# Chunked attention and two gated products on one core: operand parts and weight sums made ahead of the bursts

## The chip, the cores and the metric

The kernel runs on one core of a Trainium2 chip. The metric is the device time in microseconds (us) of one execution, the median over several runs. Five engines work side by side: TensorE (PE, with its weight loads as PEld), VectorE (DVE), ScalarE (ACT), GpSimd (POOL) and SyncE (SP). SP and POOL issue most of the transfers. Each engine runs its instructions in the order in which the program gives them to it, and waits at an instruction until what it needs is there.

## The reference

```python
# q, k, v: (8, 8, 576, 64) float32; 4608 tokens of 512 features
scores = q_c @ k_c^T / sqrt(64)                 # chunks of 64 tokens
attn   = softmax(scores, axis=-1)
x = (attn @ v_c) rearranged to (4608, 512)
x = ((x @ w_a) * (x @ w_b)) @ w_out             # d_ff 1536
out = (((x @ w1) * (x @ w2)) @ w3) @ w_out2     # d_ff 1024
```

## The kernel before

**Numbers.** A float32 operand is split into a high part and a rest, and each product is three matmuls of such parts (`SEQ`). A split is a cast on ACT (L287) and a subtraction on DVE or POOL (L288), both in `split`.

**Tiles and stages.** The 4608 tokens are nine blocks of 512. Phase 0 is the first gated product (d_ff 1536: twelve slices of 128), phase 1 the second (eight slices), with w3 and w_out2 multiplied together once. In phase 0 blocks 0 and 1 are done by `plain_step` (L1041): PE makes pa and pb (L901), DVE multiplies them (L1061 for block 1, into the tile G0p; L1065 for block 0), and `Second` (L925) multiplies with a slice of w_out (L944, twelve matmuls). The weights are converted meanwhile (`Pump`): float32 copies go to DRAM as `d`, split ones as `dw` and `dwo`, by stores on POOL. The last four plain steps are block 0's slice 11 and block 1's slices 9, 10 and 11; they are called the plain tail here. Blocks 2 to 7 run as three pairs per phase (phase 1 has four), by Strassen's scheme in `strassen_step` (L982): seven products P5, P1, P2, P6, P3, P7, P4 a slice instead of eight (L914).

**What a pair needs first.** Its x parts, by `strassen_pieces` (L605): four differences of x tiles ("formed", L616) and seven splits ("one"), each for two halves, 22 pieces in all. For the first pair also weight sums: class `Sums` (L809) loads `d` of a slice (L819, tile su), makes four sums on DVE (L827 to L830), splits two of them into w tiles and stores them as `dw[..][2]` and `[3]` (POOL) for the later pairs, which load all four parts by `load_part` (L794).

**Bursts.** After a pair's last step, and after the plain steps, `burst` (L1084) multiplies the second block's slices with w_out: twelve slices of twelve matmuls each. Beside it the x parts of the next pair are made (`Track(others, ...)`), and from its fifth slice on the attention of the pair after next goes on. `back(order)` makes the burst begin with slices 10 and 11 and then go down. The w_out slices lie in four tiles (`Outs`, L758); a slice's load (L782, tile wo) is put into the program three or four slices ahead. The first one that burst 1 loads is wo_7, for its fifth slice.

**Order of the loads.** All these loads go out on SP, one behind the other in program order; each waits at its head for its buffer and for its source's store. Attention's q, k and v loads (tiles qk and v, L181) are queued by `ask` and handed out a few at a time by `tick` and `settle`. While `state["hold"]` is true none is handed out; `burst` sets it at its start and clears it after its first slice.

Of the kernel before, what the change touches and what calls it, by code (L numbers as in the profile page):

```python
# [17 lines left out]
P = 128  # L18
NT = 512
# [91 lines left out]
def chunk_attention_two_gated_products(  # L111
# [493 lines left out]
    def strassen_pieces(x32, nm, single=False, diffs=None):  # L605
# [8 lines left out]
        def minus(a, b, name):  # L614
            t = diffs.popleft() if diffs else tmp(name, W)
            nc.vector.tensor_tensor(t, a, b, op=ALU.subtract)  # L616
            return t
# [23 lines left out]
        def one(p, kt):  # L641
# [5 lines left out]
        order = [  # L647
            (formed, "P5"),
            (formed, "P6"),
            (one, "P5"),  # L650
            (one, "P1"),
            (one, "P2"),
            (formed, "P7"),
            (one, "P6"),
            (formed, "P4"),
            (one, "P3"),
            (one, "P7"),
            (one, "P4"),
        ]
        return parts, [  # L660
            (0.7, False, lambda do=do, p=p, kt=kt: do(p, kt)) for do, p in order for kt in range(2)
        ]

# [145 lines left out]
    class Sums:  # L809
# [63 lines left out]
        def early(self, i):  # L873
            t = w_tile(6 + i, f"w{self.ph}_{self.f}_s{i}")
            self.parted(i, t)

# [207 lines left out]
    def burst(ph, j, order, gplaces, others, at, first=None):  # L1084

        n = NF[ph]
        order = back(order)
        sums = []
        state["banks"] = ("acc2", "acc3")
        track = Track(others, 2 * n // 3, engines)  # L1090
        state["hold"] = True
        parts = [ready(ph, j, order[0], gplaces) if first is None else first]
        parts.append(ready(ph, j, order[1], gplaces))
        state["outs"].ahead(3)
        for f in range(n):
            if f and f + 2 < n:
                parts.append(ready(ph, j, order[f + 2], gplaces))
            s = Second(ph, j, f, state["outs"].next(), parts[f], sums, ("rC", "rA", "rB", "rD"))
            s.part()
            s.part()  # L1100
            track.point()
            if f > 3:
                for a in at:
                    a.point()
            s.rest()
            if f == 0:
                state["pending"].rest()
                parts.append(ready(ph, j, order[2], gplaces))
                state["hold"] = False
            state["outs"].ahead(3 if f else 4)  # L1110
        track.finish()
        state["pending"], state["banks"] = None_(), ("rB", "rD")
# [88 lines left out]
    with tc.manual_schedule():  # L1201
# [83 lines left out]
        AHEAD = 5  # L1285
# [86 lines left out]
        at = None  # L1372
        for n, (T, f) in list(enumerate(order))[1:]:
# [9 lines left out]
            def point(pe=True):  # L1383
                if conv:
                    conv.point(pe)
                (at or late).point(pe)

            if T == 1:
                for i in [f + 1] if f else [0, 1]:
                    for m in range(2 if i < NF[0] else 0):  # L1390
                        store(dw[0][i][m], whole(pairs[0, i][m]).bitcast(F32), 2, nc.gpsimd)
            if n + 3 == len(order):
                at.finish()
                next_units(2)
                state["pace"] = 9
            if n + 1 == len(order):
# [5 lines left out]
        at.finish()  # L1402

# [15 lines left out]
        def block_steps(ph, sb, x, at):  # L1419
# [10 lines left out]
            for k, f in enumerate(order):  # L1430
                extra = None
                if new:
                    if k + 2 < n:
                        su[k + 2] = summed(ph, order[k + 2], k + 2)
                        su[k + 2].load()
                    extra = Track(su[k + 1].pieces() if k + 1 < n else [], 5, engines, 2.0)
# [7 lines left out]
                def freed(i):  # L1444
                    if k + 2 < n:
                        if whole_new and f + 2 >= READY:
                            return
                        if not new or i in (0, 3):
# [10 lines left out]
                if k + 1 == n and ph == 0 and sb + 1 < NSB:  # L1459
                    for a in at:  # L1460
                        a.finish()
                    next_units(sb + 2)
# [67 lines left out]
        for ph, sb in [(0, sb) for sb in range(1, NSB + 1)] + [(1, sb) for sb in range(NSB + 1)]:  # L1530
# [13 lines left out]
            elif not begins:  # L1544
                x, pieces = strassen_pieces(x32, f"{ph}{sb}", sb == NSB)
            if ph == 0 and sb == 1:
                for n_ in range(2):
                    first_sums[n_] = summed(ph, orders[ph, sb][n_], n_)
                    first_sums[n_].load()
                    for i in (0, 3):  # L1550
                        load_part(ph, orders[ph, sb][n_], i)
                pieces = pieces + first_sums[0].pieces()
# [54 lines left out]
            j, places = block_steps(ph, sb, x, at)  # L1607
# [51 lines left out]
```

## Time and profile before

| what | us |
|---|---|
| median of 3 runs | 1606.45 |
| lowest to highest | 1604.29 to 1608.12 |
| the profiled execution | 1609.44 |
| its span on the core | 1607.6 |
| PE busy | 1545.6 (96% of the span) |
| DVE busy | 859.0 (53%) |
| ACT, POOL busy | 538.4, 492.6 (33%, 31%) |

The span is what the profiler shows of the core; the execution's own time is 1.8 us longer. The plain stage fills the first 258.95 us. Burst 1 follows to 305.14, the first pair to 474.18, burst 2 to 517.32, the second pair to 674.08, burst 3 to 710.45. Shares of the whole span hide these stages, so the rows further down go stage by stage.

### The profile page before, as it was taken

To read this page: it belongs to the slowest core of one execution; us is meant where nothing else is said; L and a number is where in the kernel's file an instruction comes from. 1 tells how busy PE (TensorE), PEld (TensorE's weight loads), DVE (VectorE), ACT (ScalarE), POOL (GpSimd) and SP (SyncE) were. 2 spreads that over 40 slices of the span, in tenths; PEclk is the share of its full clock that TensorE was granted. 3 is DMA by queue.
4 is the path that set the end of the run, shared out by engine and by line. 5 is a ranking of instruction groups with operands and counts; after the bars stand their busy time and mean duration, and the time that the engine had idled before them with its cause. 6 is when DMAs were issued, how large, how long until landed. Compare 5 with 4: busy or idle time off the path is not lost.

```text
span 1607.6 us, 24155 instructions
## 1 busy us (share of the span) xinstructions
PE 1545.6 (96%) x8968; PEld 1255.6 (78%) x8968; DVE 859.0 (53%) x1384; ACT 538.4 (33%) x997; POOL 492.6 (31%) x502
## 2 busy tenths in 40 slices
PE   5799999899899999999999999999999999999998
PEld 4578787677677788887877888888878878878887
DVE  4877564677757555476776345634632432432431
ACT  3544344322233222342334323333421321421322
POOL 0323224222234111343224312224522422422422
PEclk8899999899999999999999999999999999999999
DMA  8798756677646787569985899777366266166184
GB/s 229 230 263 267 245 154 226 211 226 222 208 151 188 203 222 231 142 200 337 323 315 184 296 335 356 288 262 261 112 230 216 76 227 219 68 222 205 68 294 152
DMA packets 277014, 356.31 MB, mean 222 GB/s; under 512 B 174241, under 2 KB 194721, under 8 KB 276897
## 3 DMA queue, kind: packets, MB, share of 16 engines
q1 hardware_dynamic: 244448, 261.43, 52.7%
q0 software_dynamic: 23616, 81.80, 13.3%
q10 hardware_dynamic: 8832, 11.54, 2.1%
q8 instruction: 71, 1.16, 0.3%
q14 instruction: 47, 0.38, 0.1%
HBM read 268.70 MB, written 85.98 MB: 221 GB/s over the span
## 4 chain that ended last, share of the span: by engine, by line
PE 81%; DVE 7%; DMA 4%; issue 3%; ACT 2%; SPq 1%; POOL 1%; DVEq 0%; ACTq 0%; POOLq 0%
PE P L914 39%; PE acc L944 23%; PE pa L901 4%; PE pb L901 4%; PE wf L1189 3%; PE pb0L L901 2%; PE pa0L L901 2%; DVE xP L288 2%; DMA wo<-dwo 2%; PE x L442 1%; SPq L181 1%; PE s L390 1%; DMA qk<-in_k_dram 1%; DMA v<-in_v_dram 1%; ACT xP L287 1%
## 5 line engine op out<-in xcount | busy, mean ns | idle before, releaser
L914 PE MATMUL P<-xP,w 128*128 128x512 f32 (+1 forms) x3066 | 695.3, 380 | 13.5 <-DVE c L1034 5.2
L914 PEld LDWEIGHTS P<-xP,w 128*128 128x128 f32 x3066 | 550.7, 188 | 130.3 <-DVE c L1034 7.5
L1005 DVE TENSOR_TENSOR c<-P,c 128x512 f32<-128x512 f32 (+1 forms) x228 | 150.0, 661 | 320.4 <-PE P L914 319.7
L1001 ACT COPY c<-P 128x512 f32<-128x512 f32 (+1 forms) x228 | 128.2, 563 | 212.7 <-PE P L914 211.5
L1036 POOL TENSOR_TENSOR G<-c,c 128x512 f32<-128x512 f32 x68 | 90.7, 1334 | 312.3 <-DVE c L1005 312.2
L287 ACT CAST gh<-c 128x512 fp32r<-128x512 f32 x68 | 42.2, 621 | 325.2 <-DVE c L1034 325.1
L288 POOL TENSOR_TENSOR gl<-c,gh 128x512 fp32r<-128x512 f32 x68 | 90.7, 1333 | 191.5 <-ACT gh L287 186.0
L944 PE MATMUL acc<-gh,wo 128*128 128x512 f32 x384 | 138.2, 400 | 0.0
L1034 DVE TENSOR_TENSOR c<-P,c 128x512 f32<-128x512 f32 x68 | 47.0, 691 | 124.7 <-PE P L914 124.6
L944 PE MATMUL acc<-wo,gh 128*128 128x512 f32 x320 | 111.0, 390 | 0.5 <-ACT gh L287 0.5
L944 PEld LDWEIGHTS acc<-gh,wo 128*128 128x128 f32 x384 | 72.6, 189 | 15.7
L901 PE MATMUL pa<-xq,w 128*128 128x512 f32 x276 | 72.4, 414 | 6.3 <-DVE w L725 6.3
L288 DVE TENSOR_TENSOR xP<-xP,xP 128x512 fp32r<-128x512 f32 (+1 forms) x56 | 65.7, 1217 | 21.2 <-ACT xP L287 21.2
L944 PE MATMUL acc<-gl,wo 128*128 128x512 f32 x192 | 75.4, 393 | 0.0
L944 PEld LDWEIGHTS acc<-wo,gh 128*128 128x128 f32 x320 | 60.1, 188 | 12.9 <-ACT gh L287 1.0
L901 PE MATMUL pb<-xq,w 128*128 128x512 f32 x276 | 68.8, 398 | 0.8 <-DVE sa L1361 0.8
L901 PEld LDWEIGHTS pa<-xq,w 128*128 128x128 f32 x276 | 53.1, 197 | 19.0 <-DVE w L725 6.9
L954 ACT COPY ev<-acc 128x512 f32<-128x512 f32 x72 | 42.3, 587 | 72.5 <-PE acc L944 67.6
L944 PE MATMUL acc<-wo,gl 128*128 128x512 f32 x160 | 62.5, 390 | 0.8 <-POOL gl L288 0.8
L901 PEld LDWEIGHTS pb<-xq,w 128*128 128x128 f32 x276 | 50.9, 190 | 11.9 <-DVE sa L1361 1.3
L190 POOL DMA_DIRECT2D dw<-w x58 | 31.8, 551 | 91.0 <-DVE w L288 83.0
L408 ACT ACTIVATE e<-e 128x512 f32<-128x512 f32 x36 | 22.8, 634 | 102.2 <-DVE e L402 98.4
(163 smaller groups left out, 2368.0 us busy)
## 6 DMA issues: line engine op xcount, KB each, us to landing
w<-dw SPq DMA_DIRECT2D x175, 512.0 KB, 4.6
wo<-dwo SPq DMA_DIRECT2D x128, 512.0 KB, 4.3
dw<-w POOLq DMA_DIRECT2D x58, 512.0 KB, 4.8
w<-dw SPq DMA_DIRECT2D x59, 256.0 KB, 3.6
su<-d SPq DMA_DIRECT2D x20, 512.0 KB, 5.4
x2d<-ev POOLq DMA_DIRECT2D x36, 256.0 KB, 4.3
x<-x2d SPq DMA_DIRECT2D x36, 256.0 KB, 4.4
out_dram<-ev POOLq DMA_DIRECT2D x36, 256.0 KB, 2.9
```

Of the source, the lines that this page charges most:

```text
L190: queue.dma_start(to, src)
L287: nc.scalar.copy(dst_h, src)
L288: eng_l.tensor_tensor(dst_l, src, dst_h, op=ALU.subtract)
L901: nc.tensor.matmul(ps, w[m][:, kk // 2, wp, kk % 2], xq[kk // 2][:, kk % 2, xp], start=(begins and n == 0), stop=(ends and n == len(terms) ...
L914: nc.tensor.matmul(ps, w[:, wp, kt], x[:, kt, xp], start=(begins and n == 0), stop=(n == 5), skip_group_check=True,)
L944: nc.tensor.matmul(acc[m], a, b, start=(f == 0 and (wp, gp) == SEQ[0]), stop=(f == NF[ph] - 1 and (wp, gp) == SEQ[-1]),)
L954: nc.scalar.copy(t, acc[m])
L1001: nc.scalar.copy(t, src)
L1005: nc.vector.tensor_tensor(o, a, b, op=ALU.add)
L1034: nc.vector.tensor_tensor(g, last, c11, op=ALU.mult)
L1036: nc.gpsimd.tensor_tensor(g_place(ph, nm.split("_")[0], f, gplaces), c22, c12, op=ALU.mult)
L1189: nc.tensor.matmul(ps, t[:, gp, jj], wo2[jj // 2][:, jj % 2, wp], start=(jj == 0 and (wp, gp) == SEQ[0]), stop=(jj == NF[1] - 1 and (wp, g ...
```

## The change

It has four parts.

1. **Staged sums.** Before the last four plain steps (`n + 4 == len(order)`), `Sums` of slices 11, 10 and 9 are set up in the tiles Y0, Y1 and Y0 again, and their two split sums go into xo4, xo5 and xo6 (`staged_pieces`) and from there to `dw`. The first pair's first three steps then load four parts each by `load_part`, and load no su.
2. **Early x parts.** Before the last three plain steps, 18 of the 22 pieces of the first pair's x parts are handed to a `Track` beside these steps, with the differences in tile Y2. Burst 1 makes the other four.
3. **Beside each pair's last step** (pairs 1 and 2 of phase 0, pairs 0 to 2 of phase 1) the first eight pieces of the next pair's x parts are made; the burst makes the rest.
4. **Hold.** A burst hands out no attention loads until its slice number n-4 is done.

```diff
+    STEPS = "f5 f6 o5 o1 o2 f7 o6 f4 o3 o7 o4"
+
+    def strassen_pieces(x32, nm, single=False, diffs=None, steps=STEPS):
...
-            t = diffs.popleft() if diffs else tmp(name, W)
+            t = diffs.popleft() if diffs else None
+            if t is None:
+                t = tmp(name, W)
...
+        order = [({"f": formed, "o": one}[t[0]], f"P{t[1]}") for t in steps.split()]
...
+    def diff_tiles(name):
+        t = pool.tile([P, 4, NT], F32, tag="Y2", name=name)
+        return deque([*(t[:, i] for i in range(4)), *[None] * 4])
...
+        def staged_pieces(self, tag):
+            def stage():
+                t = pool.tile([P, 2, 4 * NT // 2], F32R, tag=tag, name=f"st{self.f}")
+                self.stage = [
+                    t[:, i].rearrange("p (o s k n) -> p o s k n", o=2, s=2, k=2) for i in range(2)
+                ]
+
+            return [
+                (1.7, None, lambda: (stage(), self.add())),
+                (0.7, None, lambda: self.parted(0, self.stage[0])),
+                (0.7, None, lambda: self.parted(1, self.stage[1])),
+            ]
...
             if f == 0:
                 state["pending"].rest()
                 parts.append(ready(ph, j, order[2], gplaces))
+            if f == n - 4:
                 state["hold"] = False
...
-        AHEAD = 5
+        AHEAD, EARLY = 5, 3
...
+                if st:
+                    st.point()
+                if xt:
+                    xt.point()
...
+            if n + 4 == len(order):
+                staged = []
+                for i in range(EARLY):
+                    su = Sums(0, NF[0] - 1 - i, dict(tag=f"Y{i % 2}"))
+                    staged.append((0.1, None, su.load))
+                    staged.append(su.staged_pieces(f"xo{4 + i}"))
+                loads = [staged[2 * i] for i in range(EARLY)]
+                pieces = loads[:2]
+                for i in range(EARLY):
+                    pieces += staged[2 * i + 1] + loads[i + 2 : i + 3]
+                st = Track(pieces, 8, engines)
             if n + 3 == len(order):
                 at.finish()
                 next_units(2)
                 state["pace"] = 9
+                got_x, got_pieces = strassen_pieces(
+                    [u.x32 for u in units],
+                    "01",
+                    diffs=diff_tiles("xd01"),
+                    steps="f5 f6 o1 o2 o3 f7 o7 f4 o4 o5 o6",
+                )
+                state["parts"] = got_x, got_pieces[18:]
+                xt = Track(got_pieces[:18], 8, engines)
...
-                    if k + 2 < n:
+                    if EARLY <= k + 2 < n:
                         su[k + 2] = summed(ph, order[k + 2], k + 2)
                         su[k + 2].load()
-                    extra = Track(su[k + 1].pieces() if k + 1 < n else [], 5, engines, 2.0)
+                    extra = Track(su[k + 1].pieces() if EARLY <= k + 1 < n else [], 5, engines, 2.0)
...
-                        if not new or i in (0, 3):
+                        if not new or i in (0, 3) or k + 2 < EARLY:
                             load_part(ph, order[k + 2], i)
...
-                if k + 1 == n and ph == 0 and sb + 1 < NSB:
+                if k + 1 == n and sb + 1 < NSB:
                     for a in at:
                         a.finish()
-                    next_units(sb + 2)
+                    if ph == 0:
+                        next_units(sb + 2)
+                    steps = "f5 f6 o5 o1 o2 f7 o6 f4 o3 o7 o4"
+                    nx, np = strassen_pieces(
+                        next_x32(), f"{ph}{sb + 1}", diffs=diff_tiles(f"xd{ph}{sb}"), steps=steps
+                    )
+                    state["parts"] = nx, np[8:]
+                    extra = Track(np[:8], 6, engines)
...
-                x, pieces = strassen_pieces(x32, f"{ph}{sb}", sb == NSB)
+                if "parts" in state:
+                    x, pieces = state.pop("parts")
+                else:
+                    x, pieces = strassen_pieces(x32, f"{ph}{sb}", sb == NSB)
...
-                    first_sums[n_] = summed(ph, orders[ph, sb][n_], n_)
-                    first_sums[n_].load()
-                    for i in (0, 3):
+                    for i in range(4):
                         load_part(ph, orders[ph, sb][n_], i)
-                pieces = pieces + first_sums[0].pieces()
```

`next_x32`, a new argument of `block_steps`, gives the x tiles of the next pair. Line numbers of the changed kernel are some 4 to 9 apart from those of before.

**SP in the plain tail.** The rows are SP's issues from the v loads of the last attention unit of the first pair (v_3) on; su_11 is the float32 copy of weight slice 11, qk_0 and v_0 belong to the next pair's attention. Before:

```order
L181 DMA v_3_2510<-in_v_dram 64x64 x6
L181 DMA v_3_2510<-in_v_dram 64x2x64
L181 DMA v_3_2510<-in_v_dram 64x3x64
L181 DMA v_3_2510<-in_v_dram 64x2x64
L181 DMA v_3_2510<-in_v_dram 64x3x64
L181 DMA qk_0_2806<-in_q_dram 32x8x32 x8
L181 DMA qk_0_2806<-in_k_dram 32x8x32 x8
```

With the change:

```order
L181 DMA v_3_2510<-in_v_dram 64x64 x6
L181 DMA v_3_2510<-in_v_dram 64x2x64
L815 DMA su_11_2744<-d_0_11_155 128x1024
L815 DMA su_10_2746<-d_0_10_154 128x1024
L181 DMA v_3_2510<-in_v_dram 64x3x64
L181 DMA v_3_2510<-in_v_dram 64x2x64
L181 DMA v_3_2510<-in_v_dram 64x3x64
L815 DMA su_9_2792<-d_0_9_153 128x1024
L181 DMA qk_0_2832<-in_q_dram 32x8x32 x8
L181 DMA qk_0_2832<-in_k_dram 32x8x32 x8
```

Three su loads now stand among the v loads and ahead of all 52 loads of qk_0, v_0, qk_1 and v_1 (these last follow in the same way, and behind them eight w loads and then wo_7). su_9 goes into the tile of su_11.

**DVE in the plain tail.** From the last attention unit's softmax (sm_3, e_3) to the plain product of block 0's slice 11. Before:

```order
L415 RECIPROCAL sm_3_2739<-sm_3_2739 128x8
L416 TENSOR_TENSOR e_3_2733<-e_3_2733,sm_3_2739 128x512
L1065 TENSOR_TENSOR sa_0_11_2712<-pb_0_11_2744,sa_0_11_2712 128x512
L1061 TENSOR_TENSOR G0p_2671<-pb_1_9_2834,sa_1_9_2832 128x512
L1061 TENSOR_TENSOR G0p_2671<-pb_1_10_2883,sa_1_10_2881 128x512
```

With the change:

```order
L416 TENSOR_TENSOR e_3_2733<-e_3_2733,sm_3_2739 128x512
L823 TENSOR_TENSOR su_11_2744<-su_11_2744 128x256
L824 TENSOR_TENSOR su_11_2744<-su_11_2744 128x256
L825 TENSOR_TENSOR su_11_2744<-su_11_2744 128x256
L826 TENSOR_TENSOR su_11_2744<-su_11_2744 128x256
L1074 TENSOR_TENSOR sa_0_11_2712<-pb_0_11_2753,sa_0_11_2712 128x512
L288 TENSOR_TENSOR st_2748<-su_11_2744,st_2748 128x2x256 x2
L823 TENSOR_TENSOR su_10_2746<-su_10_2746 128x256
L824 TENSOR_TENSOR su_10_2746<-su_10_2746 128x256
```

Four sums of su_11 stand between attention's e_3 and the product sa_0_11, and two splits of them behind it; su_9 can be loaded when the second is read. On ACT the first cast of st_2748 stands between the cast of sa_0_11 and the copy of pT_3, which PE's next attention step reads, and the second cast behind that copy.

**SP in burst 1.** The loads of burst 1's w_out slices (wo) and of the attention behind them. Before:

```order
L782 DMA wo_4_3126<-dwo_4_168 128x1024
L782 DMA wo_3_3151<-dwo_3_167 128x1024
L782 DMA wo_2_3178<-dwo_2_166 128x1024
L181 DMA qk_2_3200<-in_q_dram 32x8x32 x2
L782 DMA wo_1_3211<-dwo_1_165 128x1024
L181 DMA qk_2_3200<-in_q_dram 32x8x32 x4
L782 DMA wo_0_3233<-dwo_0_164 128x1024
L181 DMA qk_2_3200<-in_q_dram 32x8x32 x2
```

With the change:

```order
L778 DMA wo_4_3180<-dwo_4_168 128x1024
L778 DMA wo_3_3199<-dwo_3_167 128x1024
L778 DMA wo_2_3244<-dwo_2_166 128x1024
L778 DMA wo_1_3262<-dwo_1_165 128x1024
L778 DMA wo_0_3284<-dwo_0_164 128x1024
L181 DMA qk_2_3192<-in_q_dram 32x8x32 x8
L778 DMA wo_10_3327<-dwo_10_174 128x1024
L181 DMA qk_2_3192<-in_k_dram 32x8x32 x4
```

The last wo of the burst (wo_1, wo_0) now stand ahead of every qk_2 load. In burst 2 it is wo_4 to wo_10 that now go first; one load of v_0 and sixteen of qk_1 follow, and wo_11, which the burst's last slice needs, stands behind these seventeen.

## Rows read from the trace of the kernel before

**Rows 1.** The stages: length, busy us (instructions) of each engine, granted clock, DMA share, GB/s.

```profile
258.95:305.14 46.19, 40.32 (x189) 32.03 (x190) 34.00 (x47) 19.46 (x35) 20.73 (x19) 0.89 0.62 205
305.14:474.18 169.04, 160.85 (x1114) 125.76 (x1114) 117.33 (x214) 49.13 (x94) 45.28 (x49) 1.00 0.71 214
474.18:517.32 43.14, 40.01 (x192) 31.77 (x192) 33.96 (x38) 19.17 (x34) 21.98 (x18) 0.92 0.59 164
517.32:674.08 156.76, 156.60 (x1114) 125.77 (x1114) 79.21 (x152) 38.19 (x72) 32.34 (x27) 1.00 0.73 205
674.08:710.45 36.37, 36.37 (x160) 29.77 (x160) 29.17 (x27) 18.53 (x33) 21.95 (x18) 1.00 0.48 162
```

**Rows 2.** What PE waited for in burst 1: us in total, times, longest.

```profile
PE acc L944 <- DMA wo<-dwo: 3.4, 1, 3.4
PE s L390 <- DVE kT L379: 2.5, 1, 2.5
```

**Rows 3.** The same for burst 2.

```profile
PE s L390 <- DVE kT L379: 1.7, 1, 1.7
PE acc L944 <- DMA wo<-dwo: 1.4, 1, 1.4
```

**Rows 4.** A stretch of burst 1 (columns as in rows 1).

```profile
292.00:302.00 10.00, 6.62 (x17) 4.76 (x15) 6.54 (x16) 0.63 (x1) 0.85 (x1) 0.50 0.76 195
```

**Rows 5.** What SP waited for in 286 to 300 us (columns as in rows 2).

```profile
SPq L181 <- DVE kT L379: 8.8, 1, 8.8
```

**Rows 6.** SP's issues in order: start, us for the group, engine, line, operation, tiles, count.

```profile
214.54 6.37 SPq L181 DMA_DIRECT2D v<-in_v_dram  x10
220.96 4.05 SPq L181 DMA_DIRECT2D qk<-in_q_dram  x8
225.05 5.85 SPq L181 DMA_DIRECT2D qk<-in_k_dram  x8
231.21 6.77 SPq L181 DMA_DIRECT2D v<-in_v_dram  x10
238.02 4.05 SPq L181 DMA_DIRECT2D qk<-in_q_dram  x8
242.11 6.96 SPq L181 DMA_DIRECT2D qk<-in_k_dram  x8
249.59 6.45 SPq L181 DMA_DIRECT2D v<-in_v_dram  x10
...
262.04 0.32 SPq L782 DMA_DIRECT2D wo<-dwo  x1
```

**Rows 7.** A store of a float32 weight, POOL (columns as in rows 6).

```profile
225.56 0.55 POOL L190 DMA_DIRECT2D d<-cv_Y  x1
```

**Rows 8.** DMA issues in 200 to 262 us: tiles, engine, count, KB each, us to landing.

```profile
d<-cv_Y POOLq DMA_DIRECT2D x2, 256.0 KB, 4.0
```

**Rows 9.** DVE at the end of attention in the plain tail (columns as in rows 6).

```profile
238.07 0.69 DVE L416 TENSOR_TENSOR e<-e,sm 128x512 f32<-128x512 f32 x1
238.68 0.68 DVE L1065 TENSOR_TENSOR sa<-pb,sa 128x512 f32<-128x512 f32 x1
```

**Rows 10.** Weight sums, tile su, 250 to 420 us: ns min/median/max, first and last start.

```profile
L828 DVE TENSOR_TENSOR su<-su x9: 411/417/420, 286.6 to 402.1; 128x256 f32<-128x256 f32 x9
```

**Rows 11.** ACT behind rows 9 (columns as in rows 6).

```profile
239.39 0.62 ACT L287 CAST gh<-sa 128x512 fp32r<-128x512 f32 x1 [2.52 <-DVE sa L1065]
239.92 0.58 ACT L533 COPY pT<-f 128x512 f32<-128x512 f32 x1
```

**Rows 12.** A stretch with loads back to back (columns as in rows 1).

```profile
262.00:268.00 6.00, 6.00 (x27) 4.64 (x27) 1.49 (x2) 5.03 (x10) 3.91 (x6) 1.00 1.02 407
```

**Rows 13.** Loads of tile wo, 258 to 320 us.

```profile
DMA to landing us min/median/max: 3.2/3.5/5.8
```

**Rows 14.** DVE splitting an x part while POOL is idle (columns as in rows 6).

```profile
278.09 1.28 DVE L288 TENSOR_TENSOR xP<-xP,xP 128x512 fp32r<-128x512 f32 x2
```

**Rows 15.** The page's group of all such DVE subtractions: busy us, mean ns, idle before.

```profile
L288 DVE TENSOR_TENSOR xP<-xP,xP 128x512 fp32r<-128x512 f32 (+1 forms) x56 | 65.7, 1217 | 21.2 <-ACT xP L287 21.2
```

More of the change, by code (lines that the diff above doesn't have):

```diff
@@ L603, in x_quadrant @@
         return quadrants[T, K]
-    def strassen_pieces(x32, nm, single=False, diffs=None):
+    STEPS = "f5 f6 o5 o1 o2 f7 o6 f4 o3 o7 o4"
+    def strassen_pieces(x32, nm, single=False, diffs=None, steps=STEPS):
         W = HALF if single else NT
@@ L645, in one @@
             split(to[:, 0], to[:, 1], value(p, kt), nc.vector)
[L647 to L659, printed above, removed]
+        order = [({"f": formed, "o": one}[t[0]], f"P{t[1]}") for t in steps.split()]
         return parts, [
@@ L1371, in chunk_attention_two_gated_products @@
         engines.dve = engines.pe + 2.0
-        at = None
+        at = xt = st = None
         for n, (T, f) in list(enumerate(order))[1:]:
@@ L1402, in chunk_attention_two_gated_products @@
         at.finish()
+        st.finish()
+        xt.finish()
         def x2_pieces(js, got):
@@ L1417, in chunk_attention_two_gated_products, with block_steps @@
         READY = 3
-        def block_steps(ph, sb, x, at):
+        def block_steps(ph, sb, x, at, next_x32):
             single = sb == NSB
@@ L1606, in chunk_attention_two_gated_products @@
                 at.append(Track(x2_pieces(js, got), PTS * steps - 3))
-            j, places = block_steps(ph, sb, x, at)
+            nx32 = lambda: [u.x32 for u in units] if ph == 0 else got
+            j, places = block_steps(ph, sb, x, at, nx32)
             if ph == 0:
```

## The prediction

> **What bounds the kernel now.** I read the stages first, since shares of the whole span mix them. In the second pair PE is busy for 156.60 of 156.76 us and in burst 3 for 36.37 of 36.37 [rows 1]: there only PE counts, and whatever is moved beside it is free. Two stages are different. Burst 1 takes 46.19 us and burst 2 43.14, while burst 3, with the same 144 second-product matmuls and some of attention's, takes 36.37. So 9.8 and 6.8 us lie in something else than PE's work.
>
> The waits say in what. In burst 1 PE stands 3.4 us for a slice of w_out and 2.5 us for attention's transposed k [rows 2]; in burst 2 it is 1.4 and 1.7 [rows 3]. After these the granted clock is 0.50, that is 1.2 instead of 2.4 GHz, for some 10 us, in which PE is busy for 6.62 [rows 4]; at the full clock that work takes half, so the lower clock costs 3.3. Together 3.4 + 2.5 + 3.3 = 9.2 of the 9.8.
>
> Both waits have one root. SP stood 8.8 us at an attention load whose buffer DVE still read for transposing k [rows 5], and the w_out loads stood behind it. That is the reading for the whole change: SP is one line, and a load that waits holds all behind it. Of this the Trainium skill ("DMA: Bandwidth & Descriptors", Anatomy of one DMA) says that the transfer engines don't wait on semaphores, any such wait happening on the issuing sequencer; rows 5 agree, and it speaks against a change that puts a waiting load ahead of others.
>
> **Hold.** It takes the attention loads of burst 1 out from between wo_2 and wo_0. Both waits of rows 2 and the slow clock behind them, 9.2 us, would go, if nothing else made w_out late. The next part does.
>
> **Staged sums.** Three su loads (L819, now L815) enter SP's line among the last v loads, ahead of 52 attention loads, eight w loads and wo_7, the first slice that burst 1 loads. I follow that line.
>
> - SP reaches su_11 after seven of the ten v loads that began at 214.54: 214.54 + 7 x 0.637 = 219.0 [rows 6]. It must wait for the store of the float32 slice, issued on POOL at 225.56 [rows 7] and landing 4.0 later [rows 8], so to 229.6.
> - su_9 goes into su_11's tile, so it waits until DVE has read su_11 for the last time. On DVE the four sums stand behind attention's e_3, which ends at 238.07 + 0.69 = 238.8 [rows 9]. Four sums of 0.417 [rows 10] end at 240.4, the product sa_0_11 (0.68) [rows 9] at 241.1. On ACT the cast of sa_0_11 (0.62), the first cast of the sum (0.62), the copy pT_3 (0.58) and the second cast (0.62) follow [rows 11], to 243.5; DVE's second split (0.68, the nearest row's size) ends at 244.2. With an issue of its own su_9 lets SP go on at about 244.7.
> - Before, the 52 attention loads began at 220.96. Now they begin at 244.7. Their six rows add up to 4.05 + 5.85 + 6.77 + 4.05 + 6.96 + 6.45 = 34.1 us [rows 6], so they end at 278.8. Bounds: with each kind at its fastest row (32 at 0.506, 20 at 0.637) 28.9 us, with the slowest (32 at 0.87, 20 at 0.677) 41.4. I take the sum as it was, since the same loads run beside the same kind of work.
> - Then eight w loads and wo_7, 4.19 MB (six and one of 512 KB, two of 256), at the 407 GB/s of a stretch with loads back to back [rows 12]: 10.3 us. One 512 KB load alone takes 3.2 from issue to landing [rows 13], 1.9 more than its 1.3 at that rate; so wo_7 is there at 278.8 + 10.3 + 1.9 = 291.0.
>
> PE needs it after the pending slice and four of the burst's. A slice is twelve matmuls, and 160 took 36.37 [rows 1], so 2.73 each; before, that point was 258.95 + 5 x 2.73 = 272.6. In the tail PE's next attention step waits for pT_3, behind four sums and a cast more: 1.7 + 0.62 = 2.3 later. DVE also gets x pieces ahead of the products that free PE's banks, perhaps 2 more. So PE asks at 275 to 277, and waits some 14 us. What made the tail later is hidden under that wait.
>
> From 291.0 eight slices remain: 21.8; attention's scores 0.7; and the lower clock after a long wait, 3.3 as before [rows 4] (0 if it were not to fall). The burst ends at 316.8 instead of 305.14: **+11.7**.
>
> In the first pair the sums of slices 10 and 9 go. That pair takes 169.04 against the second's 156.76 [rows 1], so 12.3 for sums made beside eleven steps, 1.1 each; that of slice 11 lay in burst 1. Between 0 and -3.1 (three steps at full price with rounding); I take **-1.5**, since four w loads a step in place of two and a su load come instead.
>
> **Early x parts.** 18 pieces leave burst 1 for the plain tail. A DVE subtraction of this kind takes 0.64 while POOL is idle [rows 14], and 1.217 in the mean of the page [rows 15]. Eighteen of them (eight differences, ten splits) are 11.5 us by the one, 21.9 by the other. With the staged sums (three times 1.7 + 1.3) and three products (2.0) DVE then has 22.5 to 32.9 us of work from 238.8 on, where burst 1 began 20.2 later. In the forecast either is covered by the wait for wo_7, since the pieces that stand last are needed only by the pair; if that cover is gone, the products among them come up to 6 late. The Trainium skill ("GPSIMD Engine Reference", 1 Specifications) has POOL share its SBUF interfaces with DVE, with contention for instructions of two inputs; by that the moved work would be cheaper in the tail, where POOL does little but issue stores, than in the burst. Rows 14 and 15 agree.
>
> **Beside the last steps.** Four differences and four splits on DVE, 8 x 0.64 = 5.1 us in a step of 156.76 / 12 = 13.1 of which DVE is busy half [rows 1]. Hidden. Burst 3, with nothing idle, shows what that buys behind the pairs: **0**. At 1.217 a piece DVE would be full for one step, 3 us behind, still ahead of the pair that needs it.
>
> **Burst 2.** The waits of rows 3 (3.1) go, but wo_11, for the last slice, stands behind 17 attention loads released with slice 8: 17 x 0.506 = 8.6, and 3.5 to land [rows 13], against three slices, 8.2. PE waits 3.9 in place of 3.1: **+0.8** (at the slowest 0.87 a load +7; with no wait at all and the clock kept, -6.8).
>
> **Sum.** 11.7 - 1.5 + 0.8 = +11.0. Against the profiled execution, 1609.44, that is 1620.4; that run lies 3.0 above the median of 1606.45, so against the median **1617.4 us**. A measurement of this kernel can tell about 0.2%, 3.2 us. The forecast is slower. Its own range is 1608 to 1626: small loads 5.2 less to 7.3 more, the pair and burst 2 some 3 to either side.
>
> **Rivals.**
>
> *A, faster: the small loads don't take 0.5 to 0.9 us each when they go in one run.* An issue that nothing holds took 0.32 (the wo load) [rows 6]. If 52 go within 18 us (0.346 each), wo_7 lands at 244.7 + 18 + 12.2 = 274.9, in time. Then burst 1 is 36.4 + 0.7 = 37.1 instead of 46.2, the tail costs +2.3, the pair -1.5: -8.3, or 1598. The sign turns at 34.1 - 11.0 = 23.1 us, 0.44 a load. For it: SP is alone then, with fewer stores beside it. Against: all six rows lie between 0.506 and 0.87, whatever else ran. Chance 0.18.
>
> *B, no change: the fastest rows and every small gain.* 28.9 instead of 34.1 takes 5.2 off, the pair's whole -3.1, burst 2 at -3: 11.7 - 5.2 - 3.1 - 3 = +0.4, 1606.9. Against: k loads were never at the fast rate. Chance 0.10.
>
> *C, slower still: the 52 loads at their slowest rows,* beside the dw stores of the staged slices, which POOL now issues in this stretch: +7.3, and burst 2 worse by some 2: +20, 1627. Chance 0.06.
>
> The changed order has the loads where the change says, so a change that does nothing is no case.
>
> **How the numbers follow.** Forecast 0.66, A 0.18, B 0.10, C 0.06. Slower 0.72 (forecast and C), same 0.10, faster 0.18. The range runs from 1601, between A at 1598 and break-even, to 1626; below it lies most of A's chance, above it most of C's: under 0.2.
>
> **What would show it.** Right: SP idle for some 20 us in the tail at the su loads, its 52 attention loads from about 245 to 279; wo_7 landing near 291; PE with one wait for wo of 10 us or more in burst 1, none for kT; the clock at half behind it; burst 2 with a wait for wo alone. Wrong: burst 1 near 37 us with no wait, SP past the small loads by 265 (A); su_9 issued well before 244; or PE's time lost in the tail, at banks or pT_3, instead of at wo_7.

## The result and the profile after

The changed kernel took 1622.33 us (median of 4 runs, 1618.18 to 1626.36), the kernel before 1606.25 (4 runs on the same chip): a ratio of 1.0107, 95% interval 1.0088 to 1.0127. It is slower by 16.1 us; 11.0 were forecast. The profiled execution of the change took 1626.36, the longest of its four, with a span of 1624.6, 17.0 above that of before.

First the stages of the change, by the same columns as [rows 1]: burst 1, pair 1, burst 2.

```profile
262.88:320.56 57.68, 41.08 (x188) 32.71 (x189) 18.81 (x21) 13.02 (x23) 18.09 (x17) 0.82 0.58 184
320.56:489.68 169.12, 163.25 (x1115) 128.52 (x1114) 117.92 (x214) 49.47 (x95) 44.24 (x45) 0.98 0.69 206
489.68:533.75 44.07, 38.89 (x192) 31.20 (x191) 24.75 (x30) 16.61 (x30) 19.99 (x18) 0.96 0.48 140
```

Here and below a burst ends, and a pair begins, with PE's first product matmul of the pair, and the pair ends with its last; by this count the bursts of before end 0.16 earlier than in rows 1. Burst 1 begins at 262.88 instead of 258.95 and lasts 57.7 us instead of 46.0, in which PE is busy for 41.1. Its end, 320.56 against 304.98, carries 15.6 of the 17.0. Pair 1 is as long as before (169.1 for 169.2), burst 2 is a little longer (44.1 for 43.0), and so is pair 2 (158.0 for 156.9); burst 3 is the same (36.2). So the place is burst 1, and the next view says what stands there: PE's waits from 255 to 322 us, where [rows 2] had 3.4 for wo and 2.5 for kT.

```profile
PE acc L953 <- DMA wo<-dwo: 16.6, 1, 16.6
PE acc L953 <- DVE G0p L1070: 2.6, 1, 2.6
```

There is one wait of 16.6 us for a load of w_out, and none for kT. PE asks for it at 278.7, where 275 to 277 was forecast, and goes on at 295.3. The load is wo_7, and SP says why it is late. Its waits from 210 to 300 us:

```profile
SPq L815 <- DMA d<-cv_Y: 11.4, 1, 11.4
SPq L815 <- DVE su L823: 10.3, 1, 10.3
```

SP stands twice at the new su loads: 11.4 us until the store of the float32 slice has landed, and 10.3 us until DVE has read su_11, whose tile su_9 takes (the view names L823, the sum that DVE had just begun behind that read). The issues in order, to be set beside [rows 6]:

```profile
213.31 4.38 SPq L181 DMA_DIRECT2D v<-in_v_dram  x7
229.20 0.82 SPq L815 DMA_DIRECT2D su<-d  x2
230.06 1.94 SPq L181 DMA_DIRECT2D v<-in_v_dram  x3
242.81 0.33 SPq L815 DMA_DIRECT2D su<-d  x1
243.19 6.76 SPq L181 DMA_DIRECT2D qk<-in_q_dram  x8
249.99 9.44 SPq L181 DMA_DIRECT2D qk<-in_k_dram  x8
259.52 6.45 SPq L181 DMA_DIRECT2D v<-in_v_dram  x10
...
275.25 6.45 SPq L181 DMA_DIRECT2D v<-in_v_dram  x10
282.13 1.31 SPq L793 DMA_DIRECT2D w<-dw  x3
...
286.03 26.88 SPq L778 DMA_DIRECT2D wo<-dwo  x8
```

SP is through seven v loads at 217.7, then stands to 229.2 (su_11, su_10), then to 242.8 (su_9). The 52 attention loads go from 243.19 to 281.7, where before they went from 220.96 to 256.0. Eight w loads follow, and wo_7 is issued at 286.03, 24.0 later than before. What held su_9 is on DVE:

```profile
236.87 0.69 DVE L416 TENSOR_TENSOR e<-e,sm 128x512 f32<-128x512 f32 x1
...
238.95 0.68 DVE L1074 TENSOR_TENSOR sa<-pb,sa 128x512 f32<-128x512 f32 x1
240.84 1.95 DVE L288 TENSOR_TENSOR st<-su,st 128x512 fp32r<-128x512 f32 x2 [1.20 <-ACT st L287]
```

After e_3 (236.87) come the four sums, the product sa_0_11 and, at 240.84, two splits of su_11, which end at 242.79; su_9 is issued at 242.81. That is the line of waits as forecast.

### The profile page after: what moved, and what is told of

The parts are those of the page before. It is cut to its first block, busy times and chain, and to the rows that moved or that the text cites. A ratio compares the mean times of both kernels' runs of the same rounds, so it can differ in the third digit from the quotient of the medians.

```text
span 1624.6 us, 24173 instructions
## 1 busy us (share of the span) xinstructions
PE 1547.5 (95%) x8968; PEld 1258.8 (77%) x8968; DVE 857.8 (53%) x1384; ACT 538.4 (33%) x997; POOL 490.3 (30%) x502
## 3 DMA queue, kind: packets, MB, share of 16 engines
q0 software_dynamic: 23616, 81.80, 13.2%
## 4 chain that ended last, share of the span: by engine, by line
PE 83%; DVE 5%; DMA 5%; SPq 3%; issue 2%; ACT 1%; POOL 0%; ACTq 0%; POOLq 0%; DVEq 0%
PE P L923 38%; PE acc L953 27%; PE pa L910 4%; PE pb L910 3%; SPq L181 3%; PE wf L1199 3%; PE pb0L L910 2%; PE pa0L L910 2%; DMA wo<-dwo 2%; PE x L442 1%; DMA v<-in_v_dram 1%; PE s L390 1%; DMA w<-dw 1%; DVE c L1014 1%; PE t L519 1%
## 5 line engine op out<-in xcount | busy, mean ns | idle before, releaser
L923 PE MATMUL P<-xP,w 128*128 128x512 f32 (+1 forms) x3066 | 697.6, 381 | 11.4 <-DVE c L1014 3.5
L288 DVE TENSOR_TENSOR xP<-xd,xP 128x512 fp32r<-128x512 f32 x32 | 55.6, 1778 | 47.5 <-ACT xP L287 47.4
L190 POOL DMA_DIRECT2D dw<-w x52 | 28.4, 549 | 78.0 <-DVE w L288 68.8
## 6 DMA issues: line engine op xcount, KB each, us to landing
w<-dw SPq DMA_DIRECT2D x59, 256.0 KB, 3.8
x2d<-ev POOLq DMA_DIRECT2D x36, 256.0 KB, 3.8
x<-x2d SPq DMA_DIRECT2D x36, 256.0 KB, 4.9
out_dram<-ev POOLq DMA_DIRECT2D x36, 256.0 KB, 2.8
```

What stands on the lines that cost most here:

```text
L288: eng_l.tensor_tensor(dst_l, src, dst_h, op=ALU.subtract)
L923: nc.tensor.matmul(ps, w[:, wp, kt], x[:, kt, xp], start=(begins and n == 0), stop=(n == 5), skip_group_check=True,)
```

## The experiments

All times are medians, each with its ratio to the kernel before on the same chip; the runs are from several chips, so ratios are to be compared. Stage lengths are from the one profiled execution of each. Columns in the table: burst 1 from and to, PE's longest wait for wo in it, pair 1, burst 2 (us).

| kernel | time | ratio | burst 1 | wait | pair 1 | burst 2 |
|---|---|---|---|---|---|---|
| before | 1606.25 | | 259.0 to 305.0 | 3.4 | 169.2 | 43.0 |
| the change | 1622.33 | 1.0107 | 262.9 to 320.6 | 16.6 | 169.1 | 44.1 |
| staged sums alone | 1622.34 | 1.0109 | 259.7 to 319.9 | 21.6 | 169.4 | 41.3 |
| two slices staged | 1608.71 | 1.0025 | 259.6 to 306.6 | 7.6 | 170.2 | 43.2 |
| su loads on POOL | 1598.81 | 0.9968 | 260.8 to 299.1 | none | 161.7 | 44.4 |
| the same, hold as before | 1596.28 | 0.9944 | 262.3 to 301.5 | 2.2 | 165.8 | 37.1 |
| hold as before | 1612.94 | 1.0051 | 261.3 to 319.3 | 17.2 | 169.3 | 37.3 |
| hold alone | 1602.32 | 0.9980 | 254.6 to 295.3 | none | 172.6 | 38.8 |
| no staged sums | 1598.91 | 0.9963 | 257.2 to 293.9 | none | 170.5 | 43.5 |
| parts beside last steps alone | 1597.20 | 0.9941 | 254.3 to 298.7 | 3.3 | 168.8 | 37.6 |
| x parts only (early and beside) | 1590.83 | 0.9903 | 256.9 to 294.1 | 0.2 | 170.3 | 37.7 |
| the same, three loads at a time | 1589.47 | 0.9902 | 257.2 to 295.2 | 1.1 | 171.0 | 37.3 |
| x parts only, v on POOL | 1596.92 | 0.9950 | 258.3 to 296.1 | 0.9 | 172.5 | 37.0 |

The plain stage differs from one execution to the next. Up to burst 1 the hold alone and the parts beside the last steps alone have the plain stage of before, yet burst 1 begins at 254.6 and 254.3 in them and at 259.0 in before. Starts and ends can be compared between runs only to within some 4.6 us; lengths and waits don't carry this.

**The su loads on another queue.** Everything is as in the change, the order of the loads on SP aside.

```diff
-                    staged.append((0.1, None, su.load))
+                    staged.append((0.1, None, lambda su=su: su.load(nc.gpsimd)))
```

> The change with one edit: the three su loads of the staged sums go out on POOL's queue, SP's line is free of them. Theory (SP is one line, the 52 attention loads and wo_7 stand behind su_9): SP goes through the 52 loads from about 221 to 260 us, wo_7 lands before 272, PE has no wait for wo in burst 1, the burst lasts about 37 us from its start near 262 and ends near 300 instead of 320.6; the time falls by some 20 us, to about 1602 (1599 to 1606). Rival 1 (the tail itself, DVE's and ACT's extra work, sets the burst's end): burst 1 still ends after 315 and the time stays above 1615. Rival 2 (traffic: eight w loads and nine dw stores in the way, not SP's wait): wo_7 still lands 13 us behind the w loads, but after 280, the time stays above 1610.

1598.81 us, ratio 0.9968 (0.9946 to 0.9991). SP's line from the first of the 52 loads on (some rows left out), and PE's waits from 255 us on:

```profile
217.00 4.05 SPq L181 DMA_DIRECT2D qk<-in_q_dram  x8
...
246.70 11.38 SPq L181 DMA_DIRECT2D v<-in_v_dram  x10
...
265.09 26.32 SPq L778 DMA_DIRECT2D wo<-dwo  x8
```

```profile
PE acc L953 <- DVE G0p L1070: 3.0, 1, 3.0
```

The 52 loads begin at 217.0, the first wo is issued at 265.09, and the 16.6 us are gone; what is left is 3.0 us for a product of the plain tail. The 52 loads themselves are no quicker: they take 40.6 us by their rows, 38.2 in the change. The same sums, stores, x parts and bytes are there as in the change: neither they nor the tail make the loss, but SP's place in the line. Both rivals fall.

**One slice less.** With EARLY at 2 there is no su_9, so only the wait for su_11's source is left.

```diff
-        AHEAD, EARLY = 5, 3
+        AHEAD, EARLY = 5, 2
```

> The change with two staged slices instead of three: no su_9, so nothing waits for the reuse of su_11's tile; SP still waits for su_11's source until about 229. Theory: the 52 loads start near 232 instead of 243, everything behind them comes 11 us sooner, wo_7 lands near 284, PE's wait for it falls from 16.6 to 5 to 9 us, the burst ends near 310; the third slice's sums return to the first pair (about +1). Time about 1612 (1608 to 1615). Rival 1 (the tail's DVE work): 3 us less of it, time about 1619. Rival 2 (traffic): less by one store pair, time 1618 to 1622.

1608.71 us, ratio 1.0025 (1.0005 to 1.0045): 0.82% or 13 us less than the change. The 52 loads begin at 231.86, 11.3 earlier. PE has wo_7 at 281.3, 14.0 sooner, but asks for it 5.0 sooner too, so its wait is 7.6, or 9.0 shorter. So of the two waits on SP the one for su_9's tile makes the larger part; what is left, 7.6, stands behind the one for su_11's source, and is gone in the run before.

**The staged sums alone.** The change without parts 2, 3 and 4.

```diff
-                xt = Track(got_pieces[:18], 8, engines)
...
-                    extra = Track(np[:8], 6, engines)
...
-            if f == n - 4:
-                state["hold"] = False
+                state["hold"] = False
```

(the first of these with the lines that make its pieces)

> The staged sums alone: x parts and hold as before. Theory: SP stands at su_11's source and at su_9's tile as in the change, wo_7 lands near 294, PE waits some 14 to 17 us for it in burst 1, which ends near 317; pair 1 and burst 2 are as before within 2 us. About 1618 (1614 to 1622). Rival (the loss needs the x parts too, DVE being full in the tail): su_9 is let go before 238 or the burst ends before 311, 1612 or less.

1622.34 us, ratio 1.0109 (1.0080 to 1.0137), just above the expected range and as slow as the whole change. PE's wait for wo in burst 1:

```profile
PE acc L953 <- DMA wo<-dwo: 21.6, 1, 21.6
```

DVE has no x pieces in the tail here, and the wait for the product is 0.9 as before. The wait for wo_7 is 5.0 longer: the load is there at the same time (295.5), but PE comes to the burst 3.2 sooner and begins it at the full clock, where in the change, behind the 2.6 us of waiting, the clock is 0.58 in the mean of the first 4.0 us. So the staged sums carry the loss by themselves, and the other three parts come to nothing on balance. That balance is the next question.

**Without the staged sums.** Parts 2, 3 and 4 stay.

```diff
-        AHEAD, EARLY = 5, 3
+        AHEAD, EARLY = 5, 0
...
-                    for i in range(4):
+                    first_sums[n_] = summed(ph, orders[ph, sb][n_], n_)
+                    first_sums[n_].load()
+                    for i in (0, 3):
                         load_part(ph, orders[ph, sb][n_], i)
+                pieces = pieces + first_sums[0].pieces()
```

> The change without the staged sums: early x parts, parts beside the last steps and the hold stay; the first pair's sums are made as before. Theory: SP's line in the tail is that of before, wo_7 lands near 265, burst 1 has neither the kT nor the wo wait and keeps the clock: 37 us in place of 46.2. Time about 1599 (1596 to 1603), faster than before. Rival (the x parts in the tail or the hold cost by themselves): PE waits for products in the tail by 3 us or more, or for wo, and the time is at 1606 or above.

1598.91 us, ratio 0.9963 (0.9939 to 0.9987), as the theory had it: burst 1 has 36.7 us and no wait for wo or kT; of the x parts in the tail PE sees 1.5 us at one product instead of 0.9. Burst 2 is 43.5.

**The hold.** The change with the release of before.

```diff
-            if f == n - 4:
-                state["hold"] = False
+                state["hold"] = False
```

> The change with the hold cleared after the burst's first slice, as before. Theory: in burst 1 the queue is late at wo_7 already, so its 16 us wait stays, and no new kT wait comes since attention's k is long turned by then; burst 2 goes back to 43 us or so. Time 1620 to 1625, no difference from the change. Rival (the hold makes the loss): back to 1606 to 1612.

A miss: 1612.94 us, ratio 1.0051 (1.0029 to 1.0072), 0.56% or 9 us less than the change. In burst 1 the theory held (a wait of 17.2, none for kT). In burst 2 the late release costs 6.7, and in pair 2 another 1.0 (158.0 for 157.0). PE's wait in burst 2 of the change, and the same burst with the early release (as a window, columns as in rows 1):

```profile
PE acc L953 <- DMA wo<-dwo: 5.2, 1, 5.2
```

```profile
488.50:525.84 37.34, 37.34 (x192) 30.02 (x191) 25.04 (x30) 16.59 (x30) 19.59 (x18) 1.00 0.67 188
```

Burst 2 of the change, SP's line:

```profile
493.11 23.23 SPq L778 DMA_DIRECT2D wo<-dwo  x7
516.40 0.47 SPq L181 DMA_DIRECT2D v<-in_v_dram  x1
516.92 4.90 SPq L181 DMA_DIRECT2D qk<-in_q_dram  x8
...
525.87 0.38 SPq L778 DMA_DIRECT2D wo<-dwo  x1
```

Seven w_out loads, then 17 small loads that take 9.4 us, then wo_11, for which PE waits 5.2 us. What lets them go there is not the release itself: `turn` (L375), which transposes a unit's k, hands out that unit's loads first (`settle(self.qk_end)`), held or not. In the change attention reaches the next unit's turn in the slice at whose end wo_11 is put into the program, so the 17 loads stand ahead of it.

**The hold alone,** in the kernel before.

```diff
-                state["hold"] = False
+            if f == n - 4:
+                state["hold"] = False
```

> The kernel before with the late release of the hold alone. Theory (a load of w_out must not stand behind attention loads): burst 1 loses the 3.4 us wait for wo, since wo_1 and wo_0 stand ahead of the qk_2 loads; burst 2 gets a wait of about 5 us for wo_11 behind 17 small loads in place of 1.4. The two cancel: 1602 to 1609. Rival (the hold is a gain in both bursts): 1598 or less. Rival 2 (it is a loss by itself of 7 or more): 1612 or more.

1602.32 us, ratio 0.9980 (0.9961 to 1.0000), inside the range, though not for the reason given. The w_out loads of burst 2 in SP's line:

```profile
471.37 25.11 SPq L782 DMA_DIRECT2D wo<-dwo  x8
```

Here all eight w_out loads go ahead of the small ones (the next of those is issued at 496.5), burst 2 has no wait for wo and 38.8 us in place of 43.0. In burst 1 the wait for wo goes and the 2.5 us for kT [rows 2] stays, as does that of 1.7 in burst 2 [rows 3]: these are DVE's, busy with x parts, and not the queue's. The bursts gain 9.6 us, but most of it goes back in the pairs that follow: pair 1 takes 172.6 us (169.2 before) and pair 2 161.5 (156.9), in which DVE waits 9.9 us for late k loads, where it had no such wait before. So the late release by itself is no loss, and hardly a gain; it is a loss together with the parts made early, where a turn pulls the held loads forward at the wrong place.

**Parts beside the last steps, alone.** The change without the staged sums, the early x parts and the late release.

```diff
-        AHEAD, EARLY = 5, 3
+        AHEAD, EARLY = 5, 0
...
-                xt = Track(got_pieces[:18], 8, engines)
...
-            if f == n - 4:
-                state["hold"] = False
+                state["hold"] = False
```

> The parts beside the pairs' last steps alone, with everything else as before. Theory: burst 1 stays at 46 us with its waits for kT and wo; in burst 2 DVE has eight pieces less, turns k in time, SP doesn't stand, and both waits (3.1 us) and the slow clock go: 37.3 in place of 43.0; about 1600.5 (1598 to 1603). Rival (the prediction's 0 for this part, the burst's gain came from elsewhere): burst 2 at 42 us or more, 1604 to 1608.

1597.20 us, ratio 0.9941 (0.9913 to 0.9969), a little better than expected. Burst 1 has its old waits (3.3 and 2.5), burst 2 has 37.6 us with 0.3 of waiting, and the first three bursts of phase 1 25.3 us each in place of 25.9.

**The x parts only.** Parts 2 and 3 with the early release and no staged sums.

```diff
-        AHEAD, EARLY = 5, 3
+        AHEAD, EARLY = 5, 0
...
-            if f == n - 4:
-                state["hold"] = False
+                state["hold"] = False
```

> The x parts alone, early and beside the last steps: no staged sums, hold released as before. Theory: burst 1 about 37 us from a start near 259, burst 2 37.3 instead of 43.5, pair 1 near 170 with its sums: about 1593 (1589 to 1597), 5 to 6 under the run with the late release. Rival (burst 1 needs the hold): burst 1 above 41 us, time 1597 or more.

1590.83 us, ratio 0.9903 (0.9872 to 0.9934). Burst 1, pair 1 and burst 2 (columns as in rows 1):

```profile
256.93:294.12 37.19, 36.96 (x188) 29.72 (x189) 25.16 (x31) 13.97 (x25) 19.00 (x19) 1.00 0.81 257
294.12:464.43 170.31, 162.12 (x1115) 127.15 (x1114) 122.42 (x222) 51.47 (x99) 46.46 (x49) 0.99 0.69 212
464.43:502.10 37.67, 37.29 (x192) 30.01 (x191) 25.00 (x30) 16.59 (x30) 19.60 (x18) 1.00 0.67 184
```

Both bursts are at 37 us with the clock full. From the run before this one it differs by the early x parts alone: they take 7.2 us and both waits off burst 1 (44.4 to 37.2) without any late release; that the burst begins 2.6 later lies within the spread of starts. This version beats both kernels. The staged sums can be added to it with their loads on POOL's queue:

```diff
-                    staged.append((0.1, None, su.load))
+                    staged.append((0.1, None, lambda su=su: su.load(nc.gpsimd)))
...
-            if f == n - 4:
-                state["hold"] = False
+                state["hold"] = False
```

> The change with the su loads on POOL's queue and the hold released after the first slice as before. Theory: burst 1 stays at 37 to 39 us, since with the x parts gone DVE turns k in time and no load on SP waits for it; burst 2 falls from 44.4 to about 37.3 us; together some 7 less than with the late release: about 1592 (1588 to 1596). Rival (the attention loads between the w_out loads of burst 1 bring its wait back): burst 1 above 41 us, 1596 to 1602.

1596.28 us, ratio 0.9944 (0.9923 to 0.9966), just above the expected range. Burst 2 is 37.1, but burst 1 waits 2.2 for wo, and it begins 5.4 later than in the run before, at 262.3, with PE standing 1.6 at pT_3, 1.4 and 3.0 at products in the tail. The staged sums win 4.5 in pair 1 (165.8 for 170.3) and lose 7.4 up to the end of burst 1.

**Pair 1.** It stays near 170 us in most of these kernels; PE waits for DVE there, and DVE waits for late k loads, 6.5 us in the change (its rows are further down) and 6.3 in the run with the x parts only. Two more runs of the x parts only try to send attention's loads sooner.

```diff
-                state["pace"] = 2
+                state["pace"] = 3
```

> The x parts alone (as in the run before that had them only), with three attention loads handed out at a time in the pairs instead of two. Theory (in the first pair DVE stands for late k loads, 6 us in two waits, and the products behind it are late): the two kT waits shrink, pair 1 falls from 170 to about 165; about 1586 (1583 to 1590). Rival (the loads are held by their buffers or by w loads ahead of them, not by when they are handed out): pair 1 stays at 168 to 171, no difference.

1589.47 us, ratio 0.9902 (0.9870 to 0.9935): the time lies in the expected range, but it is the rival that came, no difference, with pair 1 at 171.0 and the waits for k still there. SP's issues follow each other with hardly a gap between 329 and 400 us, in this run as in the one before, so what is handed out sooner is not issued sooner.

```diff
     def every_other(self, to, c0, cnt, hs, s0):
+            queue = None if isinstance(self, TurnedOnPE) else nc.gpsimd
...
-                ask(to[:, c0 + c, :], hs[s0 + c * P : s0 + c * P + CH, :])
+                ask(to[:, c0 + c, :], hs[s0 + c * P : s0 + c * P + CH, :], queue)
```

(and the other `ask` of this function likewise)

> The x parts alone, with the v loads of the later pairs' attention on POOL's queue instead of SP's. Theory (in the first pair SP issues without a break, so k loads are late by what stands ahead of them): a third of the small loads leave SP's line, DVE's waits for k (6 us) go, pair 1 falls from 170 to about 164, unless POOL comes late; time about 1585 (1580 to 1590). Rival (POOL waits for v's buffers and makes g's lower parts late, or its issues cost more): PE waits for POOL's parts in the pairs, 1592 or more.

1596.92 us, ratio 0.9950 (0.9933 to 0.9967), 0.47% above the run with v on SP. DVE's waits for k are gone in pair 1, but it takes 172.5 us: DVE is busy for 133.8 us there, for 122.4 with v on SP, with the same 222 instructions.

```profile
296.11:468.65 172.54, 162.50 (x1115) 127.08 (x1114) 133.81 (x222) 51.17 (x99) 85.19 (x118) 0.99 0.67 209
```

One place where that happens, DVE and then POOL from 350 us on:

```profile
351.70 3.67 DVE L825 TENSOR_TENSOR su<-su 128x256 f32<-128x256 f32 x1
355.30 0.41 DVE L826 TENSOR_TENSOR su<-su 128x256 f32<-128x256 f32 x1
```

```profile
351.95 1.30 POOL L1047 TENSOR_TENSOR G<-c,c 128x512 f32<-128x512 f32 x1
353.20 0.56 POOL L181 DMA_DIRECT2D v<-in_v_dram  x1
353.78 1.30 POOL L288 TENSOR_TENSOR gl<-c,gh 128x512 fp32r<-128x512 f32 x1
```

A sum of 128 x 256 that takes 0.41 us next to it takes 3.67 while POOL runs one product and one subtraction of two operands close behind each other, and ends 0.3 after the second. Of the 11.4 us that DVE is busy longer in the pair, 6.5 are in these sums and 5.0 in a scaling of one operand, sm:

```profile
L414 DVE TENSOR_SCALAR sm<-sm 128x8 f32<-128x8 f32 x7 | 3.1, 437 | 0.2
L416 DVE TENSOR_SCALAR sm<-sm 128x8 f32<-128x8 f32 x7 | 8.1, 1153 | 0.2
```

(v on SP, then v on POOL). Three of the seven scalings began while POOL issued a v load and ended with the product behind it, after 1.8 to 1.9 us in place of 0.17. The reading is that the loads on POOL push its own work together and DVE pays; whether the issues hold DVE as well, or only the work behind them, no run separates. The theory on k held, and the gain went into slower DVE instructions.

## Why the prediction was right, and where not

**The main step was right, by its own rows.** "su_9 goes into su_11's tile, so it waits until DVE has read su_11 for the last time": 6.1 us were reckoned from the start of e_3 to that read's end, and 5.9 passed until su_9 was issued. "They begin at 244.7" became 243.2, with the tail 1.2 us earlier in this execution. "PE waits some 14 us" became 16.6, since wo_7 came 4.3 later and PE asked for it 1.7 behind the last of the 275 to 277 us of the forecast, and the end of burst 1, 316.8, became 320.6. The run with the su loads on POOL shows that it is this line and nothing else; the run with the staged sums alone shows that they suffice.

**Where burst 1 was sized too small: the 52 loads and the landing.** They took 38.2 us by their rows, where 34.1 was carried over "since the same loads run beside the same kind of work". The work is not the same: the first 16 took 16.2 us instead of 9.9, in a stretch in which the transfers run at 352 GB/s, where before they ran at 209; the last 36 took 22.0. The first 16 before, then both stretches of the change (columns as in rows 1):

```profile
220.96:231.20 10.24, 10.24 (x82) 8.35 (x81) 7.65 (x12) 4.46 (x9) 3.59 (x5) 1.00 0.71 209
243.10:260.00 16.90, 16.90 (x70) 13.76 (x68) 14.92 (x29) 9.14 (x18) 5.06 (x11) 0.91 1.02 352
260.00:282.00 22.00, 16.12 (x62) 12.27 (x60) 13.08 (x10) 9.31 (x17) 12.90 (x12) 0.92 0.44 111
```

Ten 512 KB stores of `dw` lie in the first stretch of the change. This is what rival C named, though it took 41.4 for the whole; that the stores are the cause is read from these rows and not shown by a run of its own. From the first w load to the landing of wo_7 13.2 us passed for 12.2. These two, 4.1 and 1.0, make the 291.0 of the forecast 295.3 (less the 1.5 that SP began sooner, and with 0.7 in gaps).

**Pair 1: -1.5 was forecast, -0.1 came.** The step took the middle between nothing and three steps at their full price. Two k loads are late there, by these waits of DVE in pair 1:

```profile
DVE kT L379 <- DMA v<-in_v_dram: 3.3, 1, 3.3
DVE kT L379 <- DMA w<-dw: 3.2, 1, 3.2
```

With SP free of the su loads the same pair takes 161.7 us, 7.4 less than in the change, with PE busy for 160.1 of them:

```profile
299.06:460.78 161.72, 160.09 (x1115) 126.15 (x1114) 119.45 (x214) 49.55 (x95) 44.15 (x45) 1.00 0.73 216
```

So the sums can be worth more than the forecast took, and in the change this did not arrive. With the loads on POOL the staged sums take 8.7 us off pair 1 beside the late release (161.7, against 170.5 without the sums) and 4.5 beside the early one (165.8 against 170.3). Why exactly the k loads come in time there was not settled: SP's line is full in both, and the two differ in more than one slot.

**Beside the last steps: 0 was forecast, and that step was wrong.** The prediction called these pieces hidden and judged their worth by burst 3, where nothing was idle. Alone they are worth 0.59% (9.5 us at 1606): DVE, with eight pieces less in burst 2, turns k in time, SP doesn't stand, and the slow clock behind goes. Of this, 5.4 is burst 2 (37.6 for 43.0) and 1.8 the bursts of phase 1. The waits were read rightly [rows 3] but credited to the hold.

**The hold: -9.2 in burst 1 was wrong in part, +0.8 in burst 2 right in size by luck.** The -9.2 did not enter the sum, being covered by the wait for wo_7. Alone the hold takes 5.4 off burst 1, since the kT wait isn't the queue's. "Both waits have one root", SP, was wrong: DVE's x parts made k late, and the early x parts, which the prediction gave no gain, remove both waits without the hold. In burst 2 the wait behind 17 loads was there as named (5.2 for 3.9), but it exists only because of the parts made early, and it is to be counted against the 37.3 us that these make possible, not against 43.0. Two errors cancelled: a gain of some 6 us in burst 2 that was not seen, given back by a wait that was priced against the old burst. That the late release also lengthens pair 2 (by 1.0 in the change) was not seen either.

**The early x parts** did little harm, and their gain of 7.2 us in burst 1 was not seen: the last product wait of the tail grew from 0.9 to 2.6 with the staged sums and to 1.5 without, and while POOL was idle the splits stayed near 0.64, as [rows 14] had them.

**The rivals.** A (small loads under 0.44 us) did not come: they averaged 0.73. The quickest rows are of 0.48 or 0.49 a load (eight k loads in 3.90 us, in the runs with two staged slices and with the staged sums alone), so no group of six or more in these runs up to 720 us reached what A needed. B fell with the same 38.2 us, where it took 28.9. A's own sum also left out the +0.8 of burst 2, which would make it 1599.

## What to carry to other kernels

A load placed early in a single queue is only early if what it waits for is ready too; before moving it, follow its buffer and its source to the engine that frees them, and price the wait by everything that stands behind it. When several parts change at once, price each against the kernel in which the others are already done: a part that is worth nothing or much alone can be the reverse beside them. And a wait that two engines share (k turned late, the queue standing) should be given to the engine whose work ends last before any part is credited with removing it.

## What the runs showed of the hardware

The granted clock after a long wait: the change, from the end of the 16.6 us wait on (columns as in rows 1).

```profile
295.30:298.00 2.70, 2.67 (x6) 2.15 (x7) 0.00 (x0) 0.00 (x0) 0.00 (x0) 0.50 0.64 259
298.00:300.60 2.60, 2.60 (x8) 1.99 (x7) 0.00 (x0) 0.00 (x0) 0.00 (x0) 0.50 0.00 0
300.60:320.50 19.90, 19.90 (x117) 16.27 (x116) 8.60 (x14) 5.03 (x9) 6.21 (x6) 1.00 0.55 167
```

After it the clock was at 0.50, 1.2 GHz, for some 5.3 us, and then full. In the kernel before, ten us at 0.50 [rows 4] follow a wait of 2.5 us and take in one of 3.4. The longer wait was the cheaper one in this respect: it cost 2.7 us by these rows, where the forecast took the 3.3 of before.

The price of a small load on SP is not fixed: in the plain tail eight q loads of 32 KB were issued in 4.04 us (x parts only) to 8.05 us (staged sums alone). The longer times stand beside large transfers, as in the rows at 209 and 352 GB/s above; no run changes these transfers alone.

DVE and POOL: a two-operand DVE sum of 0.41 us took 3.67 beside two such operations on POOL, in the rows of the last experiment. The Trainium skill ("GPSIMD Engine Reference", 1 Specifications) has the two engines share their SBUF interfaces, with contention for DVE instructions of two inputs; the rows agree. The same shows in the other kernels: in pair 1 of the run with the x parts only, eight such sums took 1.38 to 1.52 us, each begun beside one POOL subtraction and ended 0.3 us after it. In burst 1 of the change one DVE split took 4.46 us beside five POOL splits in a row:

```profile
272.97 4.46 DVE L288 TENSOR_TENSOR xP<-xd,xP 128x512 fp32r<-128x512 f32 x1 [7.26 <-ACT xP L287]
271.82 6.76 POOL L288 TENSOR_TENSOR gl_1b<-G0p,gh_1b 128x512 fp32r<-128x512 f32 x5
```

The scaling sm of the last experiment has one operand and was held as well, up to 1.88 us in place of 0.17.
